# Fused attention, MLP and top-2 experts on one core: when the first expert weights are loaded, and where the second tile table is made

## The chip, the cores and the metric

The kernel runs on one core of one Trainium2 chip. The metric is the device time of one execution in microseconds (us), given as a median over runs. The engines have their names of the profile: PE (matmuls; PEld is its weight load), DVE, ACT, POOL and SP. A name with a q behind it (SPq, ACTq, POOLq) is the engine's own issuing of instructions and DMAs.

## The reference, cut to what matters

Causal block attention (4 batches, 8 heads, 576 tokens, head size 64), then a dense MLP (512 to 2048 to 512, softplus between), then a mixture of eight experts (512 to 1024 to 512, relu between), of which each of the 2304 tokens takes the two that a noisy router picks.

```python
x = softplus(x @ w_in) @ w_out                       # every token
logits = x @ w_gate + log1p(exp(x @ w_noise)) * noise
top2 = argpartition(-logits, 2)[:, :2]; weight = softmax(logits[top2])
for e in range(8):                                   # tokens sorted by expert
    for k in range(2):
        m = top2[:, k] == e
        out[m] += weight[m, k] * (relu(x[m] @ w1[e]) @ w2[e])
```

## The kernel before, in words

All operands are split into two fp16 halves, and each product is made of three passes. The work has three stages that overlap: attention, which also converts the weights; the dense MLP over 9 groups of 256 tokens (`mlp1`, `mlp2`); and the experts, over tiles of 128 (token, expert) pairs.

**Router.** Each group ends in two calls of `route(gt)`, one for each 128 tokens (gt 0 to 17; group 8, the last, is gt 16 and 17, and the last but one is gt 14 and 15). ACT and DVE write the MLP's row into `xw` (two buffers, L411 and L412), SP turns it by a transposing DMA into `xT2` (L421, kept as `sh["turn"]`), PE makes the router's product `pg` from it (L428), DVE picks the two experts, PE makes a running count `pr` (L445), and POOL scatters the row twice to the DRAM buffer `xsc`, sorted by expert (L471). A buffer of `xw` is free again when both scatters of its tile have landed.

**Experts.** Tile t gathers its rows from `xsc` into `gx` (POOL, L850), turns them (`prep`, SP, L864; `xTe` for tiles 0 and 1), and multiplies by the weights of its expert. Weights lie converted in DRAM (`wsc`); three lanes hold one expert's pair each, `W1[l]` and `W2[l]`, 2 MB each, and tile t uses lane t % 3. `load_w` (L842) reads the expert's number and a flag from a table into registers and issues a DMA under the condition that the lane needs a new expert. The first two lanes are loaded from POOL's queue, the third from SP's, all later ones from ACT's.

**Tables.** Which tile belongs to which expert is worked out on DVE in some 40 small instructions: `table_a` for tiles 0 to 11 as soon as the first 12 router tiles are counted, `table_b` for tiles 12 on once all 18 are (`nB`, L459). Tile 12 is gathered in the pass of `run` for t = 6.

**Order.** The program is traced in Python, and a planner then orders each engine's instructions by their place in the program (`hipri` moves some forward), by their dependencies, and by its own estimate of when each is ready. Each engine executes its list in order. A dependency marked NOSYNC only fixes an order on one engine; SYNC also makes the instruction wait. While the last MLP products are still being made (`cnt["chain"]`), PE is held to the program's order, and six `pieces` of expert tiles 0 and 1 are put between them:

```python
self.pieces = [(self.l1, 0, 0), (self.l1, 0, 1), (self.l1, 1, 0), (self.l1, 1, 1), (self.l2, 0, 0), (self.l2, 0, 1)]
```

When this stretch begins, the newest `sh["turn"]` is that of gt 15. `Moe.begin` runs earlier, once gt 12 is counted. After the MLP, `tiles` loads the third lane and `run` goes through tiles 1 on, with the first product of tile t + 1 ahead of the second product of tile t.

Of the kernel before, what the change touches and what calls it, by code (L numbers as in the profile page):

```python
# [44 lines left out]
SYNC = mybir.DependencyInfo(mybir.DependencyClass.Sync, mybir.DependencyReason.DATA)  # L45
# [4 lines left out]
def body(nc, tc, i, o, stop=9):  # L50
    ctx = ExitStack()
    with ctx:
        return _body(ctx, nc, tc, i, o, stop)


def _body(ctx, nc, tc, i, o, stop):
# [10 lines left out]
    wsc = dp.tile([E, 128, 16384], F16, name="wsc")  # L67
# [45 lines left out]
    sh = dict(mm=mm, wsc=wsc, xsc=xsc, iota8=iota8, iop=iop, late=[], early=[], nA=nA, nB=nB)  # L113
# [432 lines left out]
    def mlp_quantum():  # L546

        c1, p2 = cnt["c1"], cnt["p2"]
        gr = int(CFG["gr"])
        ok1 = ok2 = far = False  # L550
        if c1 < NP * NG:
            old = 2 * (c1 // 2 - gr)
            ok1 = c1 // NP < cnt["ready"] and (c1 >= NP or 2 * c1 + 2 <= cnt["wc"])
            ok1 = ok1 and (old < 0 or p2 >= 4 * TG * (old // NP) + TG * (old % NP // 2) + TG)
        if p2 < 4 * TG * NG:
            g2, r2 = divmod(p2, 4 * TG)
            qt, t = divmod(r2, TG)
            c2 = NP * g2 + 2 * qt + 2
            ok2 = c1 >= c2 and (g2 > 0 or 4 * qt + 4 <= cnt["wc"] - 16)
            far = c1 >= min(NP * NG, c2 + int(CFG["lag" if g2 else "lag0"]))  # L560
        if ok2 and (far or not ok1):
            mlp2(g2, t, qt)
            cnt["p2"] += 1
            pipe_step()
            rpipe_step()
            return 2.6
        pipe_step()
        rpipe_step()
        if ok1:
            mlp1(*divmod(c1, NP))  # L570
            cnt["c1"] += 1
            return 2.6
        return 0
# [92 lines left out]
    mo = Moe(ctx, nc, tc, o, sh)  # L666
    began = False
    while cnt["p2"] < 4 * TG * NG or pipe or rpipe:
        if began and not cnt["chain"] and cnt["c1"] == NP * NG:
            cnt["chain"] = True  # L670
            for t in range(2):
                tc.add_manual_dep(mo.prep(t).ins, sh["turn"].ins.name, NOSYNC, reason="behind what the router needs")
        done = mlp_quantum()
        if not began and cnt["routed"] >= GA * TG:
            mo.begin()
            began = True
        if cnt["chain"] and (not done or cnt["p2"] == 4 * TG * NG - TG):
            mo.piece()
# [5 lines left out]
class Moe:  # L684
# [143 lines left out]
    def load_w(self, t, whiches=(1, 2), on="a"):  # L828

        if t >= self.end:  # L830
            return
        nc = self.nc
        k, T, E7, valid, gidx, regs = self.tab[t]
        ET = mybir.EngineType
        eng, dma = {"a": (ET.Activation, nc.scalar), "s": (ET.SP, nc.sync), "p": (ET.Pool, nc.gpsimd)}[on]
        if (t, on) not in self.lregs:
            self.lregs[t, on] = [self.rload(regs, T * n + k, eng, hi) for n, hi in ((0, 7), (1, 1))]
        e, nw = self.lregs[t, on]
        for which in whiches:
            W = (self.W1 if which == 1 else self.W2)[t % LANES]  # L840
            c0 = 0 if which == 1 else 8192
            dma.dma_start(W, self.sh["wsc"][ds(e, 1), :, c0:c0 + 8192].rearrange("a p b -> p (a b)"), cond=nw, max_dma_last_dim=2048)  # L842

    def gather(self, t):
        if t >= self.end:
# [76 lines left out]
    def begin(self):  # L922

        self.lregs = {}
        self.table_a()
        for t in range(2):
            self.gather(t)
        for t in range(2):
            self.load_w(t, (1,), "p")
        for t in range(2, 6):  # L930
            self.gather(t)
        for t in range(2):
            self.load_w(t, (2,), "p")

    def tiles(self):
        self.pb = self.ctx.enter_context(self.tc.tile_pool(name="p2b", bufs=2, side="left", reuse_waits="tile"))
        self.W1.append(self.pb.tile([128, 8192], F16, name="W1_2", bufs=1))
        self.W2.append(self.pb.tile([128, 8192], F16, name="W2_2", bufs=1))
        self.load_w(2, (1,), "s")
        while self.pieces:  # L940
            self.piece()
        self.prep(2)
        self.prep(3)
        self.load_w(2, (2,), "s")
        self.prep(4)
        self.gather(6)
        self.load_w(3)
        self.load_w(4, (1,))
        self.table_b()
        self.run(1, NT1)  # L950
        k, T, E7, valid, gidx, regs = self.tab[NT1]
        ET = mybir.EngineType
        n = self.nc.values_load(regs[0:1, 2 * T:2 * T + 1], engines=[ET.PE, ET.Activation, ET.Pool, ET.DVE, ET.SP], min_val=0, max_val=NT2,
                                skip_runtime_bounds_check_because="made on chip within these bounds")
        with self.tc.If(n > NT1 - TA):
            self.lregs = {}
            self.end = NT2
            for t in range(NT1, NT2):
                self.gather(t)
                self.load_w(t, on="s")  # L960
                self.prep(t)
            for t in range(NT1, NT2):
                self.l1(t)
            for t in range(NT1, NT2):
                self.weigh(t)
                self.l2(t)

    def run(self, t0, t1):
        for t in range(t0, t1):
            self.gather(t + 6)  # L970
            if t + DEPTH < t1:
                self.l1(t + DEPTH)
                self.load_w(t + DEPTH + LANES, (1,))
            self.prep(t + DEPTH + 3)
            self.weigh(t)
            self.l2(t)
            self.load_w(t + LANES, (2,))
# [38 lines left out]
```

## Time and profile before

| | us |
|---|---|
| median of 3 runs | 1120.35 |
| lowest and highest run | 1119.23, 1126.59 |
| the profiled execution, its own time | 1121.67 |
| its span, first to last instruction | 1119.7 |
| PE busy in the span | 1004.7 (90%) |
| mean granted TensorE clock | 0.955 |

The span is what the trace shows; 1.97 us of the execution's time lie around it. The rows of the trace count from the span's start. Up to about 600 us attention and MLP share the engines; from there to about 693 us the last MLP groups run beside the first expert tiles; then come the expert tiles alone.

### The profile page before, as it was taken

The numbers are of one execution on the slowest core, as the hardware profiler recorded it, in microseconds if no ns is written. First come the engines' busy times: TensorE is split into PE (matmuls) and PEld (weight loads), VectorE is DVE, ScalarE is ACT, GpSimd is POOL, SyncE is SP. The second block draws the span as 40 slices with busy tenths as digits, with TensorE's granted clock in tenths as the row PEclk, the third lists the DMA queues.
The fourth block names the chain that finished last, engine by engine and source line by source line (L and its number), as shares of the span: only waits on it lengthen the run. The fifth ranks groups of instructions, "written<-read, shape, count | busy, mean of one in ns | idle before, by whom it ended". The sixth has DMA issues, their size and how long they took to land.

```text
span 1119.7 us, 24473 instructions
## 1 busy us (share of the span) xinstructions
PE 1004.7 (90%) x9526; PEld 661.6 (59%) x9526; DVE 599.6 (54%) x1756; ACT 546.3 (49%) x1132; POOL 198.2 (18%) x188
## 2 busy tenths in 40 slices
PE   4677898879987988889879799999999999999996
PEld 2353455545545555556546466777777677677673
DVE  6999998677977877888756335321121121121120
ACT  6687667777877777777746331211111111111111
POOL 0233101010010101001002411322222222222111
PEclk9987999898999988989999899999999999999999
DMA  6865679999999999999985937846999348796442
GB/s 169 195 179 163 169 189 268 266 251 273 277 294 272 270 233 268 257 249 271 221 253 208 340 103 202 147 78 141 308 325 266 74 74 210 195 330 152 118 104 30
DMA packets 272518, 234.96 MB, mean 210 GB/s; under 512 B 180110, under 2 KB 217486, under 8 KB 272400
## 3 DMA queue, kind: packets, MB, share of 16 engines
q1 hardware_dynamic: 223872, 148.15, 53.8%
q0 software_dynamic: 14176, 38.17, 14.0%
q10 hardware_dynamic: 34352, 47.04, 13.2%
q8 instruction: 76, 1.25, 0.5%
q14 instruction: 42, 0.34, 0.1%
HBM read 251.60 MB, written 58.79 MB: 277 GB/s over the span
## 4 chain that ended last, share of the span: by engine, by line
PE 48%; DMA 7%; DVE 5%; ACT 4%; issue 3%; SPq 1%; POOL 0%; ACTq 0%; POOLq 0%; DVEq 0%
PE ph L74 19%; PE py L74 17%; PE l L74 9%; DMA xT<-xw 3%; DMA est<-in_wexp_dram 3%; DVE eh L514 1%; DMA pt<-P 1%; ACT eh L508 1%; PE s L238 1%; DVE P L286 1%; ACT P L280 1%; SPq L298 1%; ACT P L252 0%; ACT A L364 0%; DMA out_dram<-ys,si 0%
## 5 line engine op out<-in xcount | busy, mean ns | idle before, releaser
L74 PE MATMUL l<-xt,win 128*128 128x256 f16 x1728 | 229.8, 290 | 12.6 <-ACT R L375 5.5
L74 PEld LDWEIGHTS <-W 128*128 128x128 f16 x3936 | 223.2, 98 | 10.4 <-issue 0.9
L900 DVE SCALAR_TENSOR_TENSOR HT<-ph,HT 128x512 f16<-128x512 f32 x78 | 53.8, 691 | 324.5 <-ACT HT L899 324.5
L74 PE MATMUL l<-wout,G 128*128 128x512 f16 x864 | 212.7, 393 | 11.6 <-POOL wout L162 4.1
L74 PE MATMUL ph<-xT,W 128*128 128x128 f16 x3744 | 215.4, 219 | 0.8 <-DVE HT L900 0.8
L74 PE MATMUL py<-W,HT 128*128 128x512 f16 x936 | 208.4, 379 | 0.8 <-ACT ys L918 0.8
L74 PEld LDWEIGHTS <-win 128*128 128x128 f16 x1728 | 171.5, 103 | 51.7 <-issue 10.9
L74 PEld LDWEIGHTS <-HT 128*128 128x128 f16 x936 | 90.0, 98 | 102.5 <-issue 1.1
L74 PEld LDWEIGHTS <-G 128*128 128x128 f16 x864 | 82.4, 100 | 106.1 <-issue 20.0
L899 ACT ACTIVATE HT<-ph 128x512 f16<-128x512 f32 x78 | 46.6, 597 | 162.6 <-PE ph L74 162.6
L918 ACT ACTIVATE ys<-py,sw 128x512 f32<-128x512 f32 x39 | 26.9, 689 | 181.3 <-PE py L74 171.0
L227 PE MATMUL s<-k,q 64*128 64x128 f16 (+3 forms) x384 | 67.0, 338 | 43.6 <-ACT P L252 30.9
L286 DVE SCALAR_TENSOR_TENSOR P<-P,sm,P 128x128 f16<-128x128 f32 (+4 forms) x144 | 87.8, 624 | 21.2 <-ACT P L280 20.8
L471 POOL DMA_INDIRECT xsc<-xw,rpos x36 | 40.9, 1136 | 283.1 <-DMA xsc<-xw,rpos 83.1
L280 ACT ACTIVATE P<-P,sm 128x128 f16<-128x128 f32 (+4 forms) x144 | 80.9, 586 | 19.6 <-DMA pt<-P 11.1
L514 DVE SCALAR_TENSOR_TENSOR eh<-est,eh 128x1024 f16<-128x1024 f32 x64 | 77.6, 1218 | 23.5 <-ACT eh L508 23.4
L919 POOL DMA_INDIRECT out_dram<-ys,si x39 | 61.7, 1581 | 160.4 <-ACT ys L918 144.5
L508 ACT ACTIVATE eh<-est 128x1024 f16<-128x1024 f32 x64 | 67.2, 1053 | 41.5 <-DMA est<-in_wexp_dram 38.8
L248 DVE TENSOR_REDUCE sm<-s 128x1 f32<-128x256 f32 (+2 forms) x160 | 74.0, 475 | 18.3 <-PE s L229 13.0
L252 ACT ACTIVATE P<-s,sm 128x128 f32<-128x128 f32 (+3 forms) x128 | 66.2, 520 | 20.8 <-DVE sm L250 10.4
L227 PEld LDWEIGHTS <-q 64*128 64x128 f16 x384 | 24.1, 100 | 77.6 <-issue 59.2
L375 ACT ACTIVATE R<-l 128x512 f32<-128x512 f32 x72 | 42.1, 592 | 40.9 <-PE l L74 29.7
(201 smaller groups left out, 1000.3 us busy)
## 6 DMA issues: line engine op xcount, KB each, us to landing
W<-wsc ACTq DMA_DIRECT2D x76, 2048.0 KB
est<-in_wexp_dram SPq DMA_DIRECT2D x64, 512.0 KB
wsc<-eh SPq DMA_DIRECT2D x64, 512.0 KB
wst<-in_moe_w_in_dram SPq DMA_DIRECT2D x16, 512.0 KB
wst<-in_moe_w_out_dram SPq DMA_DIRECT2D x16, 512.0 KB
W<-wsc POOLq DMA_DIRECT2D x4, 2048.0 KB
out_dram<-zero ACTq DMA_DIRECT2D x19, 256.0 KB
rk<-in_k_dram SPq DMA_DIRECT2D x16, 288.0 KB
```

Source lines behind the costliest of these rows:

```text
L74: x = nc.tensor.matmul(*args, **kw)
L227: nc.tensor.matmul(s[hd][:, :N], Q[hs, a, 128 * T - q0:128 * T - q0 + 128], K[hs, c, :N], start=n == 0, stop=False)
L248: nc.vector.tensor_reduce(out=sm[:, hd:hd + 1], in_=s[hd][:, :wd[hd]], axis=AX.X, op=ALU.max, negate=True)
L252: nc.scalar.activation(P[:, hd, :wd[0]], s[hd][:, :wd[0]], AF.Exp, scale=esc, bias=sm[:, 2 + hd:3 + hd], accum_out=sm[:, 4 + hd:5 + hd])
L280: nc.scalar.activation(v4[:, :, 0, :], pin, AF.Copy, scale=r)
L286: nc.vector.scalar_tensor_tensor(v4[:, :, 1, :], pin, r, v4[:, :, 0, :], op0=ALU.mult, op1=ALU.subtract)
L375: nc.scalar.activation(R[:, h], ps, AF.Copy, scale=2.0 ** -21)
L508: nc.scalar.activation(hh, sv, AF.Copy, scale=sc)
L514: nc.vector.scalar_tensor_tensor(hl, sv, sc, hh, op0=ALU.mult, op1=ALU.subtract)
L899: nc.scalar.activation(HT[:, hf, 0:4], ph, AF.Relu)
L900: self.lo = nc.vector.scalar_tensor_tensor(HT[:, hf, 4:8], ph, 0.0, HT[:, hf, 0:4], op0=ALU.max, op1=ALU.subtract)
L919: nc.gpsimd.indirect_dma_start(out=self.out, out_offset=bass.IndirectOffsetOnAxis(ap=si, axis=0), in_=ys, in_offset=None, bounds_check=NTO ...
```

## The change

The four loads of the first two lanes no longer stand among the gathers in `begin`. They are traced when the ordered stretch begins, in the order W1 of tile 0, W1 of tile 1, W2 of tile 0, W2 of tile 1, still on POOL's queue, and the first of them waits until the newest turning DMA of the router has landed. The six gathers of `begin` now follow each other. `table_b` is called in `run` at t = 3 in place of ahead of the loop, which starts at t = 1.

```diff
     while cnt["p2"] < 4 * TG * NG or pipe or rpipe:
         if began and not cnt["chain"] and cnt["c1"] == NP * NG:
             cnt["chain"] = True
+            mo.lanes(sh["turn"])
             for t in range(2):
                 tc.add_manual_dep(mo.prep(t).ins, sh["turn"].ins.name, NOSYNC, reason="behind what the router needs")
...
-            dma.dma_start(W, self.sh["wsc"][ds(e, 1), :, c0:c0 + 8192].rearrange("a p b -> p (a b)"), cond=nw, max_dma_last_dim=2048)
+            l = dma.dma_start(W, self.sh["wsc"][ds(e, 1), :, c0:c0 + 8192].rearrange("a p b -> p (a b)"), cond=nw, max_dma_last_dim=2048)
+        return l
...
         self.table_a()
-        for t in range(2):
+        for t in range(6):
             self.gather(t)
-        for t in range(2):
-            self.load_w(t, (1,), "p")
-        for t in range(2, 6):
-            self.gather(t)
-        for t in range(2):
-            self.load_w(t, (2,), "p")
+
+    def lanes(self, turn):
+
+        for w in (1, 2):
+            for t in range(2):
+                l = self.load_w(t, (w,), "p")
+                if (w, t) == (1, 0):
+                    self.tc.add_manual_dep(l.ins, turn.ins.name, SYNC, reason="the router's rows go first")
...
         self.load_w(4, (1,))
-        self.table_b()
         self.run(1, NT1)
...
         for t in range(t0, t1):
+            if t == 3:
+                self.table_b()
             self.gather(t + 6)
```

## Rows read from the trace of the kernel before

**Rows 1.** The page's busy time of each engine: us, share, instructions.

```profile
PE 1004.7 (90%) x9526; PEld 661.6 (59%) x9526; DVE 599.6 (54%) x1756; ACT 546.3 (49%) x1132; POOL 198.2 (18%) x188
```

**Rows 2.** Busy time in stretches; last: granted clock, DMA share, GB/s.

```profile
620.00:630.00 10.00, 10.00 (x70) 6.68 (x69) 4.14 (x7) 5.54 (x8) 8.77 (x7) 1.00 1.03 392
630.00:640.00 10.00, 5.08 (x35) 3.14 (x33) 1.23 (x1) 3.21 (x4) 1.24 (x2) 0.88 1.05 382
640.00:650.00 10.00, 7.00 (x47) 3.11 (x48) 3.24 (x19) 1.92 (x6) 0.00 (x0) 0.61 1.09 297
```

**Rows 3.** Timeline of PE: start us, us, instruction, idle before and releaser.

```profile
632.33 2.75 PE L74 MATMUL l<-wout,G 128*128 128x512 f16 x12
642.59 0.49 PE L74 MATMUL pg<-wg,xT 128*128 128x16 f16 x12 [7.51 <-DMA xT<-xw]
642.93 5.16 PE L74 MATMUL l<-wout,G 128*128 128x512 f16 x12
648.42 0.46 PE L74 MATMUL pg<-wg,xT 128*128 128x16 f16 x12 [0.32 <-DMA xT<-xw]
...
651.72 2.78 PE L74 MATMUL l<-xt,win 128*128 128x256 f16 x24
...
669.93 2.84 PE L74 MATMUL ph<-xTe,W 128*128 128x128 f16 x48
...
688.73 0.45 PE L74 MATMUL pg<-wg,xT 128*128 128x16 f16 x12
...
704.18 5.52 PE L74 MATMUL ph<-xT,W 128*128 128x128 f16 x96 [0.80 <-DVE HT L900]
```

**Rows 4.** Timeline of POOL: loads (L842), gathers (L850), scatters (L471).

```profile
616.70 0.96 POOL L842 DMA_DIRECT2D W<-wsc  x1 [11.11 <-DVE bada L803]
617.97 1.09 POOL L850 DMA_INDIRECT gx<-xsc,gidxa  x1 [0.31 <-issue]
...
629.37 1.87 POOL L842 DMA_DIRECT2D W<-wsc  x2
651.99 1.06 POOL L471 DMA_INDIRECT xsc<-xw,rpos  x1 [20.75 <-issue]
653.36 1.07 POOL L850 DMA_INDIRECT gx<-xsc,gidxa  x1 [0.30 <-issue]
655.78 1.01 POOL L471 DMA_INDIRECT xsc<-xw,rpos  x1 [1.35 <-DMA xsc<-xw,rpos]
...
662.84 0.97 POOL L471 DMA_INDIRECT xsc<-xw,rpos  x1 [2.12 <-DMA xsc<-xw,rpos]
```

**Rows 5.** The chain that ended last, pieces on turning DMAs: start, us.

```profile
418.42 6.10 DMA xT<-xw
494.96 3.84 DMA xT<-xw
...
629.12 19.26 DMA xT<-xw
```

**Rows 6.** Timeline of SP's queue: start us, us, turning DMAs issued.

```profile
626.77 11.29 SPq L421 DMA_TRANSPOSE xT<-xw  x2
638.22 9.91 SPq L864 DMA_TRANSPOSE xTe<-gx  x2
```

**Rows 7.** Timeline of ACT: `xw` of gt 17, then the loads on its queue.

```profile
678.00 0.60 ACT L411 ACTIVATE xw<-l 128x512 f16<-128x512 f32 x1 [1.99 <-PE l L74]
...
682.17 0.12 ACTq L842 DMA_DIRECT2D W<-wsc  x1
...
686.03 0.60 ACT L899 ACTIVATE HTe<-ph 128x512 f16<-128x512 f32 x1 [2.08 <-PE ph L74]
...
692.08 1.15 ACTq L842 DMA_DIRECT2D W<-wsc  x2
```

**Rows 8.** Timeline of DVE: first and last instruction of `table_b` (38), then the next.

```profile
693.29 0.17 DVE L740 SCALAR_TENSOR_TENSOR c_eb<-a_e,nB 128x8 f32<-128x8 f32 x1
...
703.33 0.19 DVE L805 TENSOR_TENSOR gidxb<-rowb,badb 128x31 int32<-128x31 f32 x1
703.44 1.29 DVE L900 SCALAR_TENSOR_TENSOR HT<-ph,HT 128x512 f16<-128x512 f32 x2
...
728.82 0.69 DVE L900 SCALAR_TENSOR_TENSOR HT<-ph,HT 128x512 f16<-128x512 f32 x1 [6.73 <-ACT HT L899]
```

**Rows 9.** Timeline of POOL: the first gather that uses `table_b`.

```profile
743.38 1.05 POOL L850 DMA_INDIRECT gx<-xsc,gidxb  x1 [4.83 <-DVE si L879]
```

## The prediction

> **What bounds the kernel now.** I read the page's busy shares first: PE works for 90% of the span, no other engine for more than 59% [rows 1]. So an edit counts only where PE stands still or runs slowly, and the next view is the table of stretches around the edit, where the reader should look for the one break in a full PE. From 600 us on PE is full but for 630 to 650 us, where it works 5.08 and 7.00 of 10 us each, at a granted clock of 0.88 and 0.61, while the DMA engines are full, at 382 and 297 GB/s [rows 2]. Third, PE's timeline says who ends the break: the router's product of gt 14 waits 7.51 us for its turned row, that of gt 15 another 0.32, and the twelve MLP matmuls between take 5.16 us where the twelve before took 2.75: TensorE went on at 1.2 of 2.4 GHz after the pause [rows 3]. Fourth, the chain of waits: the turning DMA of gt 15 is 19.26 us of it, while two earlier ones took 6.10 and 3.84 [rows 5]. Fifth, the queues tell why: POOL issued its first 2 MB load at 616.70 and its last two from 629.37 [rows 4], and SP issued the two turning DMAs from 626.77 on and needed 11.29 us for it [rows 6]. They met the loads.
>
> **The four loads behind the turning DMA.** What is removed: four loads of 2.10 MB, 8.39 MB, and the collision. From 632.33 to 651.72 PE took 19.39 us [rows 3]. Undisturbed the same work is: twelve matmuls, 2.59 (half of 642.93 to the end of the busy time at 648.10); the product of gt 14, 0.34 (642.59 to 642.93); twelve more, 2.59; the rest from 648.42 to 651.72, 3.30, which ran at full clock. Sum 8.82, so at most **10.57 us** come back.
>
> Are the rows turned in time then? PE asks for gt 14 at 632.33 + 2.59 = 634.9 and for gt 15 at 634.9 + 0.34 + 2.59 = 637.9. The turning starts at 626.77 [rows 6] and 629.12 [rows 5]; with 3.84 to 6.10 us each [rows 5] they land by 630.6 to 632.9 and 633.0 to 635.2. Both ends are early enough, by 2 us at least, so I take the whole 10.57.
>
> What is late next? All that follows comes 10.57 us earlier, so the weights of tile 0 are due at 669.93 - 10.57 = 659.4 [rows 3]. POOL wakes at 635 at the latest, issues four loads in some 4 us (0.96 for one, 1.87 for two, [rows 4]), and 8.39 MB need 22 us at 382 GB/s, 28 at 297 [rows 2]. So the first load lands near 642 and the last near 658 (664 at the lowest rate); the later three are due after 659.4, at their pieces. At 382 GB/s nothing waits.
>
> The Trainium skill speaks against this edit: "DMA: Bandwidth & Descriptors", section "Rules for kernel authors", has DMAs issued early and waited for late. By that rule alone the move gains nothing and only spends slack. The trace bears out the other side here: the early issue collides with a DMA that is due sooner [rows 3, 5].
>
> **The new wait.** On POOL it stands ahead of the scatters of gt 14 and 15 and of the gather of tile 6. These need the count after the same turning, at about 651.99 - 10.57 = 641.4 [rows 4], so the wait itself delays none. But the scatters now go into POOL's queue behind up to 8.39 MB. No row shows a scatter there, so I bound it: landing at once, or after the loads. At the late end the first lands near 659, the second is issued at 659.5, and the last 7.06 later (655.78 to 662.84, [rows 4]), at 666.6, landing some 3.5 after that (the spacing of the rows), at 670.1. ACT may write `xw` of gt 17 only then; its turn would be 678.00 - 10.57 = 667.4 [rows 7]. It would be 2.7 us late. Behind it on ACT stand the hidden halves of tile 0, for which PE has a second buffer, and the turning of gt 17: at most 671.4 + 6.1 = 677.5, against 688.73 - 10.57 = 678.2 [rows 3]. So the late end costs PE 0 to 1 us, the early end nothing. I take 0.4, since the queue is most likely served in order.
>
> In a sentence of the Trainium skill by itself: the same page, section "Two DMAs through the same engine are not ordered", has descriptors of one queue start in order, which would give the late end; no run here shows it yet.
>
> The six gathers in a row, the moved register reads and the changed return value cost nothing: POOL sat idle 20.75 us before 651.99 [rows 4].
>
> **The table two tiles on.** `table_b` is 38 DVE instructions from 693.29 to 703.5, and only behind it DVE takes the hidden halves for which PE has waited 0.80 us [rows 8, 3]. With lower priority than the halves of tiles 2 and 3 it lets them pass at the first seam, after 0.4 us or less. Gain **0.80 us**; the other end is 0, if the planner puts it into the same idle stretch whole. I take 0.80, since the instructions are separate. If it goes as one block of 10.2 us at t = 3, DVE's pause of 6.73 [rows 8] is exceeded by 3.5 us once; PE has another buffer and a second product of a tile in between, so that hides it. Its first user is the gather at 743.38 [rows 9], now near 732, over 15 us after such a block.
>
> **Sum.** 10.57 + 0.80 - 0.37 = 11.0 us. The profiled execution took 1121.67 (span 1119.7 and 1.97 around), so 1110.7 on its scale; the median is 1.32 lower, so **1109.4 us**, 0.98% down. With the ends of the terms (gain 9.8 to 11.6) 1108.8 to 1110.6; another 1 us for run-to-run shifts.
>
> **Rivals.**
> First, **three of the loads don't wait** (the change doesn't do what it says). Only the first has the dependency, and POOL's order does go by readiness: a load came at 616.70 ahead of a gather that was traced before it, and the gather of tile 6 ahead of scatters traced long before [rows 4]. Against it: on ACT's queue the load of W1 for tile 4 could have gone when the first product of tile 1 was evacuated, near 686, but it came at 692.08 together with the load traced before it [rows 7]; loads seem to keep their order among themselves. Price: 6.29 MB plus 1.6 MB of gathers in place of 10.0 end 5.4 us sooner (2.10 / 0.387), and the turning with them: gain 5.4 + 0.8 = 6.2, or only 3 if the loads also slip behind the gathers. 1114 to 1117.5.
>
> Second, **the scatters' delay reaches PE**. At 297 GB/s the loads end at 664, the last scatter lands at 675.3, `xw` of gt 17 is 7.9 late and its turning is done at 682.7, 4.5 after PE wants it. Net gain 11.4 - 4.5 to 7.9: 1113.5 to 1117; between this and the forecast it is 1111 to 1114. For it: 297 is the rate while turning DMAs run too. Against: in 620 to 640 us the rate was 382 to 392 [rows 2].
>
> Third, on the other side, **the collision is handed on to the turning DMAs of tiles 0 and 1**. They are issued right behind gt 15's [rows 6] and may still run when the loads start. If they are slowed as gt 15's was (it landed 5 us after the loads' 10.0 MB, begun at 617, must have ended near 643), tile 0's lands at 658 + 5 = 663, a stall of 3.6; at 297 GB/s at 669, a stall of 9.8, and after it 2.6 us of half clock as in [rows 3]. 12.4 lost against 11.4 won: 1121.4, slower than before by 1. It starts to cost when `xTe` of tile 0 lands after 659.4, and turns the sign after 668.4. Against: they start before the loads, and free ones take 3.84 to 6.10 [rows 5].
>
> **How the numbers follow.** Forecast (loads wait in order, scatters hidden): 0.74, at 1108 to 1111. First rival 0.08, second 0.10, third 0.06, other 0.02. From 1107.6 to 1115 lie the forecast, the near half of the second rival and part of the first, 0.85 in all. 1% is about what a measurement can tell from no change, and 1% down is 1109.15, just inside the forecast's own range: I give 0.40 of its 0.74 to faster by over 1%, the rest and nearly all of the rivals to within 1%. Slower by over 1% would take 22 us of loss, for which no row has a price: 0.03.
>
> **What would show it.** In the changed profile: four POOL loads after about 634, none before; no PE wait on the turned rows of gt 14 and 15, and a granted clock of 1.00 through 620 to 660; the full DMA stretch moved to 636 to 660; the first `xTe` product near 659; no wait of 0.80 for the halves at tile 3. Wrong if loads still stand near 620, if ACT waits for the scatters before gt 17's `xw` long enough that PE waits for `pg`, or if PE waits for `xTe`.

## The result, and the profile after

| | before | after | ratio, 95% interval |
|---|---|---|---|
| median, us (runs) | 1122.76 (4) | 1111.96 (4) | 0.9887, 0.9839 to 0.9936 |
| lowest and highest | 1119.23, 1126.59 | 1103.73, 1118.24 | |
| profiled execution, its span | 1121.67, 1119.7 | 1112.65, 1110.7 | |
| mean granted clock | 0.955 | 0.965 | |

The change makes the kernel 1.1% faster; the forecast was 0.98%, and 1109.4 us on the scale of the runs shown then. The two spans are 9.0 us apart. Where they differ is read best from PE, which executes the same 9526 matmuls in the same order in both kernels. I cut its time in three. The front ends with the matmuls ahead of the last but one group's router products. The **block** goes from the twelve `wout` matmuls ahead of gt 14's product to the 24 `win` matmuls behind the two counts (632.33 to 651.72 in [rows 3]). The rest runs from there to the last matmul.

| us | before | after |
|---|---|---|
| start of the block | 632.33 | 633.80 |
| the block | 19.39 | 9.24 |
| end of the block to the last matmul's start | 458.93 | 458.93 |
| from there to the end of the span | 9.04 | 8.69 |

So 10.15 us come from the block, the rest up to the last matmul gave nothing, the tail 0.35, and the front happened to end 1.47 us later: 9.03 in sum. The first view of the changed kernel is again the table of stretches (busy us of PE, PEld, DVE, ACT, POOL, then granted clock, DMA share, GB/s), which answers to [rows 2]:

```profile
620.00:630.00 10.00, 10.00 (x71) 6.68 (x69) 4.38 (x6) 6.33 (x8) 8.17 (x7) 1.00 0.56 142
630.00:640.00 10.00, 10.00 (x89) 6.72 (x87) 3.61 (x13) 5.04 (x10) 2.70 (x3) 1.00 0.94 231
640.00:650.00 10.00, 9.44 (x71) 6.30 (x70) 5.00 (x39) 3.77 (x7) 1.98 (x2) 1.00 1.03 392
650.00:660.00 10.00, 10.00 (x72) 6.86 (x71) 2.14 (x2) 4.29 (x5) 3.50 (x3) 1.00 1.00 369
```

PE is full but for 0.56 us, and the clock stands at 1.00 throughout; the DMA engines are full from 640 to 660 us, where before they were from 620 on. PE's timeline, which answers to [rows 3], has no wait for a turned row. It has a small one that was not there:

```profile
633.80 2.75 PE L74 MATMUL l<-wout,G 128*128 128x512 f16 x12
636.39 0.45 PE L74 MATMUL pg<-wg,xT 128*128 128x16 f16 x12
636.70 2.75 PE L74 MATMUL l<-wout,G 128*128 128x512 f16 x12
639.28 0.45 PE L74 MATMUL pg<-wg,xT 128*128 128x16 f16 x12
639.59 1.03 PE L74 MATMUL l<-xt,win 128*128 128x256 f16 x8
641.18 0.18 PE L74 MATMUL pr<-roh,tri 128*128 128x8 f16 x1 [0.56 <-DVE rw L463]
...
661.26 0.94 PE L74 MATMUL ph<-xTe,W 128*128 128x128 f16 x14
...
695.50 4.68 PE L74 MATMUL ph<-xT,W 128*128 128x128 f16 x81 [0.80 <-DVE HT L902]
```

The queues tell the cause. SP needs 3.58 us for the two turning DMAs that took 11.29 [rows 6], and POOL has no load ahead of them (L843 are loads, L471 scatters; compare [rows 4]). But the four loads do not follow each other: the planner put scatters between them. (For the first load the profile names a turning DMA of `xTe`, issued just behind, as what released it. The program makes it wait for gt 15's, and held_again names that one for the same load: 3.28 us, DMA xT<-xw.)

```profile
628.24 3.58 SPq L421 DMA_TRANSPOSE xT<-xw  x2
631.99 2.93 SPq L866 DMA_TRANSPOSE xTe<-gx  x2
```

```profile
628.79 2.05 POOL L852 DMA_INDIRECT gx<-xsc,gidxa  x1 [0.30 <-issue]
635.53 0.95 POOL L843 DMA_DIRECT2D W<-wsc  x1 [4.69 <-DMA xTe<-gx]
637.30 0.91 POOL L843 DMA_DIRECT2D W<-wsc  x1 [0.82 <-PE pg L74]
643.33 1.07 POOL L471 DMA_INDIRECT xsc<-xw,rpos  x1 [5.12 <-issue]
644.39 0.91 POOL L843 DMA_DIRECT2D W<-wsc  x1
651.58 1.57 POOL L471 DMA_INDIRECT xsc<-xw,rpos  x1 [6.28 <-DMA xsc<-xw,rpos]
653.15 0.91 POOL L843 DMA_DIRECT2D W<-wsc  x1
658.14 1.03 POOL L471 DMA_INDIRECT xsc<-xw,rpos  x1 [4.08 <-ACT A L364]
664.73 1.00 POOL L471 DMA_INDIRECT xsc<-xw,rpos  x1 [5.56 <-DMA xsc<-xw,rpos]
```

On ACT `xw` of gt 17, which the scatters could have held up, waits for PE as in [rows 7]. On DVE `table_b` runs in one piece, right behind the copy of `nB` and ahead of the hidden halves, as in [rows 8]; the wait of 0.80 us behind it has stayed. First ACT, then DVE:

```profile
669.32 0.60 ACT L411 ACTIVATE xw<-l 128x512 f16<-128x512 f32 x1 [1.99 <-PE l L74]
```

```profile
684.62 0.17 DVE L741 SCALAR_TENSOR_TENSOR c_eb<-a_e,nB 128x8 f32<-128x8 f32 x1
...
694.66 0.19 DVE L806 TENSOR_TENSOR gidxb<-rowb,badb 128x31 int32<-128x31 f32 x1
694.77 1.30 DVE L902 SCALAR_TENSOR_TENSOR HT<-ph,HT 128x512 f16<-128x512 f32 x2
```

### The profile page after: what moved, and what is told of

The parts are those of the page before. It is cut to its first block, busy times and chain, and to the rows that moved or that the text cites. A ratio compares the mean times of both kernels' runs of the same rounds, so it can differ in the third digit from the quotient of the medians.

```text
span 1110.7 us, 24476 instructions
## 1 busy us (share of the span) xinstructions
PE 999.6 (90%) x9526; PEld 661.4 (60%) x9526; DVE 599.9 (54%) x1756; ACT 546.5 (49%) x1132; POOL 200.0 (18%) x188
## 4 chain that ended last, share of the span: by engine, by line
PE 43%; DVE 3%; DMA 2%; ACT 1%; issue 1%; SPq 0%; POOL 0%; POOLq 0%; ACTq 0%; DVEq 0%
PE ph L74 19%; PE py L74 17%; PE l L74 6%; DMA est<-in_wexp_dram 1%; DVE eh L514 1%; DMA xT<-xw 0%; DMA out_dram<-ys,si 0%; SPq L298 0%; DVE G L372 0%; DVE P L286 0%; ACT A L367 0%; ACT A L364 0%; ACT eh L508 0%; ACT P L252 0%; ACT R L375 0%
## 5 line engine op out<-in xcount | busy, mean ns | idle before, releaser
L74 PE MATMUL l<-wout,G 128*128 128x512 f16 x864 | 209.6, 389 | 14.0 <-POOL wout L162 5.0
L471 POOL DMA_INDIRECT xsc<-xw,rpos x36 | 42.1, 1169 | 281.6 <-DMA xsc<-xw,rpos 99.7
```

Of the source, the lines that this page charges most:

```text
L74: x = nc.tensor.matmul(*args, **kw)
```

## The experiments

The theory: the gain is the collision of the early loads with the turning DMA of gt 14 and 15, and the wait on the first load is what ends it. The rivals: the move of the table has a share; the loads would be harmless at their new place without a wait; a delay of the scatters or of the turning DMAs of tiles 0 and 1 takes part of the gain back. In the table, "rest" is the time from the end of the block to the last matmul. Ratios are against the kernel before on the same chip, and stand where a kernel ran six times or more.

| kernel | time, us | ratio, 95% | start | block | rest |
|---|---|---|---|---|---|
| after_again | 1113.61 | 0.9909, 0.9874 to 0.9945 | 632.68 | 9.25 | 458.91 |
| table_alone | 1124.55 | 1.0006, 0.9981 to 1.0031 | 631.28 | 21.24 | 458.94 |
| table_held | 1110.70 | 0.9875, 0.9843 to 0.9907 | 637.78 | 9.25 | 457.89 |
| held_again | 1111.42 | one run | 632.99 | 9.24 | 458.57 |
| no_wait | 1122.01 | 0.9980, 0.9951 to 1.0008 | 638.48 | 9.24 | 458.93 |
| no_wait_b | 1115.58 | one run | 626.73 | 19.33 | 458.93 |
| no_wait_c | 1108.52 | one run | 629.47 | 9.25 | 458.93 |
| two_early | 1119.04 | one run | 638.53 | 10.76 | 458.92 |
| three_early | 1116.89 | one run | 630.25 | 16.95 | 458.92 |
| loads_first | 1113.30 | one run | 630.39 | 9.41 | 462.76 |
| turns_late | 1116.46 | one run | 633.06 | 9.25 | 463.43 |

The start of the block lies anywhere from 626.7 to 638.5 us, and in one and the same kernel too (no_wait, no_wait_b and no_wait_c are one). A single time can't rank these kernels, then; the block and the rest can.

### The change again, and its halves

**after_again** is the changed kernel itself.

> The changed kernel once more, to measure by itself how much of its time is the edit. My theory: all of the gain lies between PE's twelve MLP matmuls ahead of the router's product of gt 14 and the 24 matmuls after the counts, a block that took 19.39 us before and 9.24 in the first profile after; what comes ahead of it (up to 600 us) wanders by some us from run to run, and what comes after it is the same to 0.02 us. So: block 9.2 again, and a ratio to the kernel before of 0.991 (gain 10.15 of 1120). The rival, that the edit also slows or speeds the front part, expects the front again 1.5 us later than before's and a gain of 8.7.

It holds: 0.9909, and a block of 9.25 us.

**table_alone** is the kernel before with only the call of `table_b` moved.

```diff
-        self.table_b()
         self.run(1, NT1)
...
         for t in range(t0, t1):
+            if t == 3:
+                self.table_b()
             self.gather(t + 6)
```

> The kernel before with only the table's call moved to t = 3. My prediction gave this 0.80 us. The theory after the first profile: the planner puts the 38 instructions into the same idle stretch of DVE wherever the call stands, as none of the hidden halves is ready then; so nothing changes, PE's wait of 0.80 us at tile 3 stays, the block stays near 19.4, ratio 1.000 within the noise of a few tenths of a per cent. The prediction's step expects the wait gone and 0.999.

The ratio is 1.0006. Its engines execute the same instructions in the same order as those of the kernel before: the planner puts the table's instructions where they were. Its profile is thus a second one of the kernel before, with a block of 21.24 us and a wait of 0.89 us for the hidden halves. The changed kernel, too, differs from the kernel before in the order of POOL's instructions alone. The move of the table is no edit at all, and the whole gain is the loads'.

**table_held** is the changed kernel with the table held behind the hidden halves of tile 3, which is what the move was taken for in the prediction; **held_again** is the same kernel on another chip.

```diff
-            V.scalar_tensor_tensor(c_e, first, -128.0, n_e, op0=ALU.mult, op1=ALU.add)
+            x = V.scalar_tensor_tensor(c_e, first, -128.0, n_e, op0=ALU.mult, op1=ALU.add)
+            self.tc.add_manual_dep(x.ins, self.lo.ins.name, NOSYNC, reason="behind the hidden halves of tile 3")
```

> The changed kernel, in which the first instruction of the table must also come behind the last hidden half of tile 3 on DVE. If the 0.80 us wait is the price of the table standing ahead of the halves, the wait goes and PE's distance from the block to the last matmul is 0.80 shorter than in the changed kernel (1101.97 less 643.04 = 458.93 there, so 458.1), the table ends near 711 and the first gather with it, near 735, isn't later. Rival: the table as a block of 10 us delays the halves of tile 4 and PE waits there instead; the distance stays 458.9 or grows. Time 0.9 us under the changed kernel, less than the runs can show.

> The change with the second table held behind the hidden halves of tile 3, looked at again on another chip. All theories: block of 9.2 us, no wait of 0.80 us for the halves of tile 3, 457.9 us from the end of the block to the last matmul (458.9 in the changed kernel). It is here for the block's start, which was 637.8 us in its profile and 632 to 634 in those of the changed kernel: if this is chance of the execution, it lies anywhere between 631 and 639 here; if holding the table does it, at 636 or later again, though the instruction lists ahead of the block are the same.

The wait is gone: on PE the two products of tiles 2 and 3 run on as one (192 matmuls), and on DVE the table begins behind the last half of tile 3. These are PE's and DVE's timelines of table_held:

```profile
693.09 10.88 PE L74 MATMUL ph<-xT,W 128*128 128x128 f16 x192
```

```profile
704.64 0.69 DVE L903 SCALAR_TENSOR_TENSOR HT<-ph,HT 128x512 f16<-128x512 f32 x1 [1.99 <-ACT HT L902]
...
705.75 0.16 DVE L741 SCALAR_TENSOR_TENSOR c_eb<-a_e,nB 128x8 f32<-128x8 f32 x1
```

The rest is 1.04 us shorter in the one profile and 0.36 in the other (458.93 less 457.89 and 458.57; the second has a pause of 0.38 us in the first product of tile 4, which the trace puts on issuing). The time has the lowest ratio of all timed kernels, 0.9875, and beats the kernel before; from the changed kernel, with 0.9909 in the same comparison, the intervals don't part it. The late start of its block was chance, since held_again begins at 632.99.

### The wait

**no_wait** takes the wait from the loads and leaves the place where they are traced. **no_wait_b** and **no_wait_c** are the same kernel, profiled twice more.

```diff
-                l = self.load_w(t, (w,), "p")
-                if (w, t) == (1, 0):
-                    self.tc.add_manual_dep(l.ins, turn.ins.name, SYNC, reason="the router's rows go first")
+                self.load_w(t, (w,), "p")
```

> The changed kernel without the one dependency of the first load on the turning of gt 15; the loads are still traced late. If the wait is what counts, the loads go out right behind or among the gathers, as before, the turning DMAs meet them and PE's block is back at 17 to 22 us with the half clock in it: ratio to the kernel before 1.000, to 1.002 since the last loads go out some us later than before. If the later place in the program counts by itself (rival), the block stays near 9 and the ratio near 0.991.

By its times the wait counts: 0.9980 without it against 0.9909 with it (after_again), and the two intervals don't meet. But the first profile contradicted the theory: a block of 9.24 us with no wait for a turned row, and still a median almost that of the kernel before. Hence the two further profiles.

> The kernel without the wait (the loads traced where the change traces them, none of them made to wait), looked at again, because its median (1122.0 us) and its profiled execution (block of 9.24 us, no PE wait on a turned row) do not fit together. Theory of a race: in each execution it is open whether SP issues the turning DMAs of gt 14 and 15 before or after POOL issues the loads behind the first. Where the turning comes first by 1 us or more, the block takes 9.2 us as in the earlier profile; where the loads come first or together with it, PE waits for the row of gt 15 or of both, the block takes 15 to 21 us, and the span is 6 to 12 us longer for the same start of the block. Over two looks at least one of the second kind is expected. Rival: the loads do no harm at this place at all, the block takes 9.2 us in both looks, and the median lies high because the front ends late (block start at 636 us or later) or because time is lost behind the block (more than 461 us from its end to the last matmul).

> The same kernel as no_wait_b, a second look of the same kind. Theory of a race: the block takes 9.2 us if the turning DMAs of gt 14 and 15 are issued before the loads behind the first, and 15 to 21 us if not. Rival: 9.2 us in each look, and the time is lost ahead of the block or behind it.

One profile has the stall, the other hasn't. What differs is behind which of the two turning DMAs the three loads come. First POOL, SP, PE and the chain of no_wait_b:

```profile
620.38 1.04 POOL L852 DMA_INDIRECT gx<-xsc,gidxa  x1 [0.30 <-issue]
621.43 2.76 POOL L843 DMA_DIRECT2D W<-wsc  x3
```

```profile
621.17 4.18 SPq L421 DMA_TRANSPOSE xT<-xw  x2
```

```profile
629.32 0.45 PE L74 MATMUL pg<-wg,xT 128*128 128x16 f16 x12
...
640.84 0.49 PE L74 MATMUL pg<-wg,xT 128*128 128x16 f16 x12 [8.46 <-DMA xT<-xw]
```

```profile
623.52 17.27 DMA xT<-xw
```

Gt 14's turning DMA went out 0.26 us ahead of three loads and was in time; gt 15's, at 623.52, went out behind them and landed 17.27 us later. In no_wait_c the same three loads come 0.25 us behind gt 15's turning DMA, and PE waits for neither. Its queues, POOL's and then SP's second turning DMA alone:

```profile
626.52 2.76 POOL L843 DMA_DIRECT2D W<-wsc  x3
```

```profile
626.27 1.40 SPq L421 DMA_TRANSPOSE xT<-xw  x1
```

The profile of no_wait is of the second kind, with its loads 0.25 us behind gt 15's turning DMA. That the median of no_wait (12 runs, 1117.01 to 1130.92) comes from executions that mostly stall is argued from these three profiles, not shown run by run.

**two_early** and **three_early** put the wait on the third and on the fourth load in place of the first.

```diff
-                if (w, t) == (1, 0):
+                if (w, t) == (2, 0):
```

```diff
-                if (w, t) == (1, 0):
+                if (w, t) == (2, 1):
```

> The changed kernel with the dependency on the third load, so that two of the four (4.2 MB) go out early: the first ahead of the gathers, the second behind them, just as the turning of gt 14 starts near 628. Collision as a dose: 2.1 MB of the second load and a gather are then left, some 6 us at 385 GB/s, so the turned row of gt 14 lands near 635 to 637 and that of gt 15 near 640; PE wants them 2.6 and 5.5 us after the block's start. Block 9.5 to 11.5 us, clock not halved. Were the collision a matter of yes or no, the block would be near 19.

> The same with the dependency on the fourth load: three go out early, 6.3 MB, two of them behind the gathers. By the dose, 4.2 MB more than nothing are left when the turning starts, 11 us: gt 14 lands near 640 to 642, gt 15 near 645, a wait of 4 to 6 us and the half clock after it; block 14 to 17. This is also the price of my first rival (three loads that don't wait), which I put at a gain of 3 to 6 us.

In both, gt 14's turning DMA goes out just ahead of the free loads and is in time, where the expectations had it late, and gt 15's falls behind one load and a gather (two_early) or behind two loads (three_early). The chains of the two, in this order:

```profile
635.32 10.63 DMA xT<-xw
```

```profile
627.03 15.39 DMA xT<-xw
```

With no_wait_b that is a dose: behind one, two and three fresh loads gt 15's turned row takes 10.63, 15.39 and 17.27 us from issue to landing, and the block 10.76, 16.95 and 19.33 us. The third load adds less than the second. As the price of the first rival, three_early says a gain of 2.44 us (19.39 less 16.95) where the prediction had 3 to 6. The load that these kernels issue some 9 to 10 us ahead of the turning did no harm by itself.

The kernel before does not fit this order of issue. There gt 15's row took 19.26 us [rows 5] although it was issued 0.25 us ahead of the last two loads [rows 4], and gt 14's, issued 2.60 us ahead of them, kept PE waiting for 7.51 us [rows 3]; table_alone repeats both (8.18 and 1.38 us of waiting on PE). What that kernel has and the others lack is a second load 5.51 us ahead of the turning, on POOL's timeline:

```profile
621.26 0.95 POOL L842 DMA_DIRECT2D W<-wsc  x1
```

So to be issued first is enough where one load, 9 to 10 us earlier, and the gathers stand ahead; with a second load among the gathers it was not. That this load makes the difference was not tried by itself.

### The two delays

**loads_first** raises the loads' priority, so that they precede every scatter, as the prediction had assumed.

```diff
-            mo.lanes(sh["turn"])
+            with tc.high_priority(offset=3000):
+                mo.lanes(sh["turn"])
```

> The changed kernel with the four loads moved forward in the planner's priority, so that they go out in a row ahead of the four scatters of gt 14 and 15, as my prediction had it; the planner had put scatters between them. If a scatter waits in POOL's queue for all loads ahead of it, the first lands at the loads' end near 660, the last is issued near 668 to 670 and ACT's write of the row of gt 17 waits for it by 2 to 4 us; PE loses 0 to 1 us, or 4 to 8 by my second rival. If scatters pass the loads, they are done by 657 and nothing waits.

Here the first scatter does stand behind all four loads. POOL's and ACT's timelines:

```profile
634.04 2.66 POOL L844 DMA_DIRECT2D W<-wsc  x3 [0.97 <-PE pg L74]
640.09 1.07 POOL L471 DMA_INDIRECT xsc<-xw,rpos  x1 [3.39 <-issue]
659.83 1.00 POOL L471 DMA_INDIRECT xsc<-xw,rpos  x1 [18.67 <-DMA xsc<-xw,rpos]
...
666.78 0.97 POOL L471 DMA_INDIRECT xsc<-xw,rpos  x1 [2.27 <-DMA xsc<-xw,rpos]
```

```profile
669.91 0.60 ACT L411 ACTIVATE xw<-l 128x512 f16<-128x512 f32 x1 [5.82 <-DMA xsc<-xw,rpos]
```

The chain gives the first scatter's time from issue to landing:

```profile
640.09 18.95 DMA xsc<-xw,rpos
```

The second rival is real in this order, at 3.83 us of the rest (462.76 less 458.93): PE waits 0.54 us for a hidden half, and later 2.30 us for the turned rows of tile 2. Behind that wait the granted clock is 0.72 in 690 to 695 us, and the 192 matmuls of tiles 2 and 3 take 12.51 us, against 10.88 in table_held; in turn the wait of 0.80 us for the hidden halves at tile 3 is gone.

**turns_late** makes the turning DMAs of tiles 0 and 1 wait until the first load has landed, so that they run among the other loads.

```diff
-            mo.lanes(sh["turn"])
+            l = mo.lanes(sh["turn"])
...
+                tc.add_manual_dep(x.ins, l.ins.name, SYNC, reason="among the loads")
```

> The changed kernel with the turning of tiles 0 and 1 held until the first load has landed (near 642), so that it runs among the other three loads, as in my third rival. If a turning DMA crawls while loads run and lands about 5 us after their end, as that of gt 15 did before, tile 0's is ready at 661 to 666, PE wants it at 661.3: a wait of 0 to 5 us. If it only shares (double its free time), it lands by 656 and nothing waits.

The third rival's own place stays free. SP and PE:

```profile
643.36 10.61 SPq L868 DMA_TRANSPOSE xTe<-gx  x2
```

```profile
660.53 2.84 PE L74 MATMUL ph<-xTe,W 128*128 128x128 f16 x48
...
675.89 4.33 PE L74 MATMUL ph<-xTe,W 128*128 128x128 f16 x48 [1.98 <-DVE HTe L904]
```

`xTe` of tile 0 was issued with two loads ahead of it and a third 0.3 us behind, and the product 18.22 us after the block, as in every other kernel, found it there. In no_wait the same DMA goes out as the last of the four loads is being issued; SP's and POOL's timelines:

```profile
637.47 14.27 SPq L866 DMA_TRANSPOSE xTe<-gx  x2
```

```profile
635.52 2.76 POOL L843 DMA_DIRECT2D W<-wsc  x3
```

There too the product comes 18.22 us after the block, at 665.95, and waits for nothing.

The loss in turns_late, 4.5 us of the rest, is elsewhere: the last two scatters went out at 663.47 and 670.41, ACT's `xw` of gt 17 waited 7.26 us for them, PE 1.98 us behind that, and its next 48 matmuls took 4.33 us where they take 2.84 (granted clock 0.70 in 675 to 680 us). These two are 3.47 of the 4.50 us.

## Why the prediction was right, point by point

**The bound** was read rightly: the break in PE between 630 and 650 us, made by the loads' collision with the turning, was all that the change could win. That one block carries the whole difference.

**The block, 10.57 us.** Measured 10.15 (19.39 less 9.24). The missing 0.42 is most of the new wait of 0.56 us at 641.18, for DVE's part of the router: from the start of gt 15's product to the block's end it is 3.76 us (639.28 to 643.04) where the sum had 3.30. The undisturbed block of 8.82 us was summed from matmuls alone. But where PE no longer stands still, DVE's small router steps for gt 14 must be done between its product at 636.39 and the end of the eight `win` matmuls at 640.62, beside two dense evacuations (L368 and L372), which the chain of the changed kernel shows among them:

```profile
636.81 1.22 DVE R L368
...
639.46 1.12 DVE G L372
...
641.13 0.07 DVE rw L463
```

The trace of before has such a wait at the group ahead, on PE's timeline:

```profile
582.84 0.18 PE L74 MATMUL pr<-roh,tri 128*128 128x8 f16 x1 [0.62 <-DVE rw L433]
```

The sum should have had such a term.

**Turned in time.** Both rows were, with 3.58 us of issuing. The early bulk loads cost 7.7 to 10.1 us in three_early and no_wait_b (16.95 and 19.33 against 9.25), because a small DMA that is due at once was issued behind them. The Trainium skill's "DMA: Bandwidth & Descriptors", section "Rules for kernel authors", would have the loads early. These runs go against it here.

**What is late next.** Nothing waited for weights, as forecast. But the four loads did not go out within 4 us: they were issued from 635.53 to 653.15, with scatters between them.

**Table, 0.80 us: this step failed.** The prediction took it "since the instructions are separate", with "let them pass at the first seam". They stayed in one piece in the same idle stretch, its other end of 0: the planner gave the same order wherever the call stood, and table_alone is the same program. That its estimate of when each is ready does this is argued, not shown. The price itself was about right: with the table held behind the halves the wait goes, and the rest is 1.04 us shorter (table_held; 0.36 in held_again).

**Scatters, 0.4 us.** In the changed kernel they cost 0, for a reason that the prediction did not have: it assumed the four loads in a row, and the planner let each scatter go out between them. A scatter still waited for the loads ahead of it (the second went out at 651.58, 6.28 us after POOL was free, once the first had landed), but the last went out at 664.73, 4.59 us ahead of ACT's write at 669.32. Its late end was timed well for the row order (first scatter landing near 659, last issued at 666.6; loads_first has 659.04 and 666.78, with a block that began 1.9 us earlier), and sized too low: 0 to 1 us against 3.83, because the turning of tile 2 hangs on the same scatters, by way of ACT's late write and the product behind it (in the chain it runs from 674.95 for 14.12 us), and a stretch at a lower clock followed. In loads_first the first scatter, behind all four loads in POOL's queue, took 18.95 us. The Trainium skill's "DMA: Bandwidth & Descriptors", section "Two DMAs through the same engine are not ordered", has descriptors of one queue start in order, and loads_first agrees.

**Sum.** 10.15 + 0 - 0 in place of 11.0. The difference of 0.85 is the table (0.80) and the wait on `pr` (0.42), less the scatters that cost nothing (0.37), and the spread of the front's end, several us, is larger than all of them. That the medians moved by 10.80 us, nearly the 11.0 of the sum, is luck for that reason; the block's 10.15 is not. On the ratio the forecast of 0.9902 lies inside both intervals of the changed kernel.

**Rivals.** The first (three loads don't wait) is out: the three followed the first in the changed kernel, as they keep their order. The second is out in the changed kernel and real where the loads have their way (loads_first). The third is out: `xTe` was issued at 631.99, ahead of the first load, and its product came at 661.26, which is 18.22 us behind the block as before. In no_wait `xTe` was issued as the last load was, and the product came no later.

## What to carry to other kernels

A bulk load issued early is not free if a small DMA with a near deadline is issued behind it: look at what each queue issues just after it, and make the bulk wait for the small one explicitly, since without that it differs from execution to execution which small DMA the loads come ahead of. Before costing the move of a call in the source, compare the instruction lists, for a planner may put it back; and where several executions begin the disputed stretch at different times, compare the stretch, not the total.

## What the runs showed that was not expected

- A turning DMA issued 0.25 us ahead of three loads (6.29 MB, on another queue) was in time (no_wait_c); behind them the same one took 17.27 us (no_wait_b). In the kernel before, with a second load 5.51 us ahead of the turning, it took 19.26 though two loads came 0.25 us behind it.
- In the kernel before and in the five profiles of no_wait, no_wait_b, no_wait_c, two_early and three_early, the free loads behind the gathers come 0.24 to 0.26 us after the issue of one of the two turning DMAs. In table_alone a gather ends at that moment (627.02 and 2.04 us long, against 628.81), and the loads follow one gather later. In the changed kernel, too, gathers end there (628.79 and 2.05 us long, against a turning DMA issued at 630.59). So what varies is which gather, or load, meets which turning DMA. What ties POOL to that moment no run here shows.
- The front's end moved by 11.8 us between profiles (626.73 to 638.53), by as much (626.73 to 638.48) within one kernel, no_wait, while the rest kept to 0.03 us in all kernels where the order behind the block was untouched. The cause was not looked for.
- After a wait of 1.81 us in two_early the granted clock stayed at 1.00, after 1.98 us in turns_late it fell to 0.70 in the next stretch of 5 us. These runs don't show why.
